# Moving VectorE work between units: one more added pair of q-k products, one more early set of down-weight sums, and a later deadline for V's sums

## The chip, the cores and the metric

The kernel runs on one NeuronCore of a Trainium2 chip. The metric is the device time of one execution in microseconds (us). Before the change the median of three runs is 715.35 us (715.16 to 716.04). A profile of one more execution comes with it; that execution took 715.07 us.

## The reference

Everything is bfloat16; x is 2048 rows of 1024 values. The output mixes an attention branch and a gated MLP branch row by row.

```python
g = _sigmoid((x * gate_w).sum(-1, keepdims=True))
# A: 32 heads of 32, each row looks at itself and 7 earlier rows, 2 apart
q, k, v = split(x @ wqkv)                       # wqkv 1024 x 3072
idx  = pos[:, None] - 2 * arange(8)[None, :]    # negative: masked with -1e9
logits = einsum("bhsd,bhswd->bhsw", q, k[idx]) * 32 ** -0.5
a = einsum("bhsw,bhswd->bhsd", softmax(logits), v[idx]) @ wo
# B: hidden width 3584
b = (gelu(x @ w_gate) * (x @ w_up)) @ w_down
return g * a + (1 - g) * b
```

## The kernel before

**Units.** The rows are handled as two halves `s` of 1024 rows. All projections of x are cut into 78 *units*. A unit makes two 128-column tiles of one projection for one half. It does so by a seven-product scheme (Strassen-Winograd): the 2 x 2 blocks of the weights and of x are combined by additions beforehand, and seven block products of four 128x512 matmuls each replace eight. So a unit is 28 matmuls, all issued by `Unit.mm` (L354). Units 2 to 9 make q and k of half 0, 10 to 17 q and k of half 1 (`t` counts eight tile pairs in each half, so unit 2 + 8s + t is the pair (s, t)), 18 to 25 make V, and 26 to 77 make gate and up. After unit 77 comes the down stage: two calls of `down`, in which TensorE works at L1074 and L1107.

**Order in a unit.** For unit b the main loop issues, to TensorE: product 1 of b, products 7 and 3 of unit b-1, product 5 of b, then a *slot* in which head sums may be made, products 2 and 6 of b, and last product 4 of unit b-1. VectorE adds product 5 to the banks that 7 and 3 left (L400, one instruction for each unit). Product 4 of the same unit accumulates into one of these banks, so TensorE can't start it before L400 is done.

**VectorE's background work.** Everything else on VectorE is handed out by a planner while the program is written (`bg`, `run_bg`, `due`). Each task is a generator that yields the cost in us of what it has just issued. In each unit the planner adds 4.7 (4.8 from unit 26 on) to a credit, plus 1.6 or 0.8 if the slot held reductions; what was left over carries on, at most 0.3 of it if positive, all of it if negative. It then steps the task with the lowest priority number whose time has come, as long as the credit is above 0.3. Tasks with the same number go in the order in which they were entered. `due(n, task)` and `at(n, fn)` run at the start of unit n, ahead of its L400, and charge nothing to the credit. So VectorE's order in unit b is: what is forced at its start, L400 of unit b-1, what `at_end` holds, and the planner's tasks.

**q-k products.** The task `qk_prods` (priority 2, from unit n+2 on, due at n+4 for a pair made in unit n) multiplies q by the eight shifted k for three blocks of 256 rows: two blocks in one instruction (L599, 4096 elements) if the credit is over 1.5, else one (L592, 2048 elements). When an odd t is done, the products of t-1 and t are summed over each head's 32 values on TensorE: `reduce_mm` (L604) issues four 128x512 matmuls with 32 columns of ones for each product, so 24 for a pair of tiles, in the slot of a later unit. For a pair in `ADDED` VectorE first adds the two tiles' products (L637: one instruction of 4096, one of 2048 elements), and 12 matmuls are enough; before, only the last pair, (1, 7), is there, as a task of priority 1.9. The products of the next pair start only when the reductions of the pair before are issued. `softmax` takes the head sums on VectorE in a front part (priority 1) and, after the exponential on ScalarE, `softmax_back` (priority 3: L726 sum, L728 reciprocal, L729, L731).

**Down-weight sums.** `t_forms` combines the down and output weights for the down stage in nine sets q of 2 k-tiles: one subtraction of 2048 elements (L892), two of 1024 (L895), and four stores of 256 KB through GpSimd's queue (L898). Set q is loaded by `tf_load` on the SP queue into `R_TF[q]`, an offset in KB in the one big SBUF tile `arena`. Sets 0 to 4 may be formed from units 2, 3, 6, 8 and 9 on, with priority 6; `tf_close` at the end of unit 13 forces what is left of them, sets the priority to 4.5 and issues `load_v`, V's weights, into 92 to 108 KB. Set 5 lies at 16 KB, is loaded at unit 19, may start at unit 20 and is forced by `tf_done` at unit 23; sets 6 to 8 come from unit 28 on. Other users of 16 to 24 KB are q's weights up to unit 17 and, from unit 24 on, `sums_pair` of the first gate and up weights (L314, priority 1, four instructions that each write 2 KB of it).

**V's sums.** `sums_v` (L540, priority 2, from unit 16) makes four weight sums of 2048 elements for V; it is due at unit 18.

Of the kernel before, what the change touches and what calls it, by code (L numbers as in the profile page):

```python
# [23 lines left out]
SJ = AC // NJ  # L24
# [10 lines left out]
R_Z = (194.5, 196.5)  # L35
R_ZH = 90
R_EX = (194.5, 81, 50, 81, 84)
R_ATTN = 73
R_E = 81
R_GW = 81  # L40
# [6 lines left out]
R_ST = 178  # L47
R_P5B = 198.5
R_RAW = (0, 8)
R_TF = (64, 92, 100, 108, 92, 16, 92, 100, 108)  # L50
R_S = (16, 24)
R_O = (36, 32)
R_VB = (40, 48.25)
# [9 lines left out]
def _win_ap(src: bass.AP, dims):  # L63
    return AP(src.tensor, src.offset, [list(src.ap[0])] + [list(d) for d in dims])
# [3 lines left out]
def kernel(  # L68
# [20 lines left out]
    NT = KT  # L89
# [12 lines left out]
    def reg(kb, n):  # L102
        o = int(kb * KB)
        return arena[:, o:o + n]

    def reg3(kb, a, b):
        return reg(kb, a * b).rearrange("p (a b) -> p a b", a=a)
# [4 lines left out]
    def regf(kb, n):  # L112
        return reg(kb, 2 * n).bitcast(F32)
# [23 lines left out]
    with tc.manual_schedule(engines={mybir.EngineType.PE, mybir.EngineType.DVE, mybir.EngineType.Activation,  # L137
# [63 lines left out]
        def flat(a):  # L201
            return a.rearrange("p a b -> p (a b)")
# [210 lines left out]
        now = [0]  # L413
# [17 lines left out]
        def bg(gen, prio, wake):  # L431
            t = Task(gen, prio, wake)
            tasks.append(t)
            tasks.sort(key=lambda t_: t_.prio)
            return t
# [41 lines left out]
        def at(n, fn):  # L477
            hooks.setdefault(n, []).append(fn)
# [7 lines left out]
        def due(n, t):  # L486
            at(n, t.finish)

        Q0 = 2
# [40 lines left out]
        def load_v():  # L530
            for k0 in (0, HK):
                nc.sync.dma_start(out=wv[:, k0:k0 + HK, :],
                                  in_=A_wqkv[k0 * P:(k0 + HK) * P, 2 * D:3 * D].rearrange("(k p) n -> p k n", p=P))

        def sums_v():
            L11, L12 = wv4[:, 0:HK, :, 0:4], wv4[:, HK:KT, :, 0:4]
            L21, L22 = wv4[:, 0:HK, :, 4:8], wv4[:, HK:KT, :, 4:8]
            for o_, a, b_, op in ((sv[0], L21, L22, ALU.add), (sv[1], sv[0], L11, ALU.subtract),
                                  (sv[2], L12, sv[1], ALU.subtract), (L21, L11, L21, ALU.subtract)):
                TT(out=o_, in0=a, in1=b_, op=op)  # L540
                yield 1.14

        def v_forms(t):
# [9 lines left out]
        NQKV = len(units)  # L553
# [18 lines left out]
        prod = [reg3(o, NWIN, AC) for o in pr_off]  # L572
        attn_all = reg3(R_ATTN, NBLK, SC)
        mask = reg3(R_MASK, NWIN, SJ)
# [11 lines left out]
        def prod_tile():  # L586
            k = pr_n[0] % 6
            pr_n[0] += 1
            return prod[k]

        def qk_mult(dst, q, k):
            TT(out=dst, in0=q.rearrange("p (o s) -> p o s", o=1).to_broadcast([P, NWIN, AC]),  # L592
               in1=_win_ap(k, [[-DIL, NWIN], [1, AC]]), op=ALU.mult)

        def pair_at(a, b):
            return _win_ap(reg(a, NWIN * AC), [[int((b - a) * KB), 2], [1, NWIN * AC]])

        def qk_mult2(dst, q, k, sq, sk):
            TT(out=dst, in0=_win_ap(q, [[sq, 2], [0, NWIN], [1, AC]]),  # L599
               in1=_win_ap(k, [[sk, 2], [-DIL, NWIN], [1, AC]]), op=ALU.mult)  # L600
# [4 lines left out]
                                 start=start, stop=stop)  # L605

        ND = BPS - 1
        ADDED = {(1, 7)}
        LGB = 5
        reduced, front, prods = [0], set(), {}  # L610

        def qk_prods(u, s, t):
            while reduced[0] < NT * s + t - t % 2:
                yield None
            assert ND == 3 and pr_n[0] % 3 == 0
            k = pr_n[0] % 6
            out_ = [prod_tile() for _ in range(ND)]
            a = 0
            while a < ND:
                if a == 0 and credit[0] > 1.5:  # L620
                    qk_mult2(pair_at(pr_off[k], pr_off[k + 1]), u.T[:, 0, 0:AC], u.T[:, 1, 0:AC], AC, AC)
                    a += 2
                    yield 2.21
                else:
                    qk_mult(out_[a], u.T[:, 0, a * AC:(a + 1) * AC], u.T[:, 1, a * AC:(a + 1) * AC])
                    a += 1
                    yield 1.14
            prods[t] = out_
            if (s, t) in ADDED:
                bg(qk_add(s, t), 1.9, now[0])  # L630
            elif t % 2:
                slotq.append((1.6, lambda: (qk_reduce(s, t - 1, prods[t - 1]), qk_reduce(s, t, out_))))

        def qk_add(s, t):
            for a, b in ((0, 3), (2, 5)):
                u, v = ((pair_at(pr_off[i], pr_off[i + 1]) if a == 0 else reg(pr_off[i], NWIN * AC)) for i in (a, b))
                TT(out=u, in0=u, in1=v, op=ALU.add)  # L637
                yield 2.21 if a == 0 else 1.14
            slotq.append((0.8, lambda: qk_reduce(s, t - 1, prods[t - 1], 2)))

        def qk_reduce(s, t, out_, m=1):
            assert s == 0 or t > 0 or front == {0, 2}
            for a, pr in enumerate(out_):
                reduce_mm(bank(LGB + a), pr, t == 0, t + m == NT)
            reduced[0] += m
            if t + m == NT:
                if s == 0:
                    bg(softmax(0, 2, LGB, 0), 1, now[0])
                    bg(softmax(2, 1, LGB + 2, 1), 1, now[0])
                else:  # L650
                    bg(softmax(BPS, 3, LGB, 2), 1, now[0])
# [42 lines left out]
        ready = set()  # L694
        md = consts.tile([P, 4, SJ], F32, name="md")

        def softmax(a, cnt, b0, e):
            ee = regf(R_EX[e], cnt * SC)
            e4 = ee.rearrange("p (a w s) -> p a w s", a=cnt, w=NWIN)
            sw = ee.rearrange("p (a w s) -> p a s w", a=cnt, w=NWIN)  # L700
            lg = banks[:, b0:b0 + cnt, :]
            src = lg.rearrange("p a (w s) -> p a w s", w=NWIN)
            bc = lambda t_: t_.rearrange("p a (o s) -> p a o s", o=1).to_broadcast([P, cnt, NWIN, SJ])
            if a == 0:
                TT(out=src[:, 0], in0=src[:, 0], in1=mask, op=ALU.add)
                yield 0.6
            m = md[:, (0, 2, 0, 3, 0)[e]:(0, 2, 0, 3, 0)[e] + cnt, :]
            assert e < 2 or ready >= {2: {0, 1, 2}, 3: {0, 1, 2}, 4: {4, 5, 6}}[e]
            V.tensor_reduce(out=m, in_=lg.rearrange("p a (w s) -> p a s w", w=NWIN), axis=AX.X, op=ALU.max)
            yield 0.55 * cnt + 0.05  # L710
            TT(out=e4, in0=src, in1=bc(m), op=ALU.subtract)
            yield 0.55 * cnt + 0.05
            front.add(a)
            actq.append(lambda: softmax_exp(a, cnt, ee, e4, sw, m, bc))
# [3 lines left out]
        def softmax_exp(a, cnt, ee, e4, sw, m, bc):  # L718
            nc.scalar.activation(out=ee, in_=ee, func=ACT.Exp, scale=scale)
            bg(softmax_back(a, cnt, ee, e4, sw, m, bc), 3, now[0] + 1)  # L720
# [91 lines left out]
        at_slot(Q0 + 8, lambda: (gate_chunk(3, bank(1)), bg(gate_task(1), 0, Q0 + 8)))  # L812
        due(Q0 + NT + 1, bg(late_form3(), 1, Q0 + 8))
        TFE = Q0 + 12
        due(Q0 + 2 * NT, bg(sums_v(), 2, TFE + 2))
        for s in range(2):
            for t in range(NT):
                n_ = Q0 + NT * s + t
# [44 lines left out]

        NP = 2
        NQ = NK // NP
        N1, N2 = 5, 6
        TB = Q0 + 2 * NT + 1
        TC = NQKV + 1

        def tf_set(q):  # L870
            return [reg3(R_TF[q] + NP * k, NP, SC) for k in range(4)]

# [8 lines left out]
        def t_forms():  # L881
            for q in range(NQ):
                tf_q[0] = q
                if q in (N1, N2):
                    tft.prio = 3.9 if q == N1 else 4.5
                    tasks.sort(key=lambda t_: t_.prio)
                while now[0] < (Q0 + (0, 1, 4, 6, 7)[q] if q < N1 else 1 + (TB if q < N2 else TC)):
                    yield None
                r11, r12, r21, r22 = tf_set(q)
                n_ = NP * SC  # L890
                both = _win_ap(flat(r11), [[n_, 2], [1, n_]])
                TT(out=both, in0=_win_ap(flat(r12), [[2 * n_, 2], [1, n_]]), in1=both, op=ALU.subtract)  # L892
                yield 1.14
                for o_, a, b_ in ((r22, r22, r11), (r21, r21, r22)):
                    TT(out=flat(o_), in0=flat(a), in1=flat(b_), op=ALU.subtract)  # L895
                    if o_ is r21:
                        for k, t in enumerate((r11, r22, r12, r21)):
                            nc.gpsimd.dma_start(out=t_d[k][:, NP * q:NP * q + NP, :], in_=t)  # L898
                    yield 0.61

        for q, b in ((2, 2), (3, 4), (4, 5)):
            at(Q0 + b, lambda q=q: tf_load(q))
        at(TB, lambda: ([tf_load(q) for q in range(N1, N2)], spill_load(1)))
        at(TC, lambda: [tf_load(q) for q in range(N2, NQ)])
# [3 lines left out]
            while tf_q[0] < N2:  # L908
                tft.step()

        at(NQKV - 3, tf_done)

        def tf_close():
            while tf_q[0] < N1:
# [362 lines left out]
        def head():  # L1277
            xs, f = xf[0], []
            for i, o in enumerate((R_ATTN, R_PROD)):
                for m in range(2):  # L1280
# [122 lines left out]
```

## Time and profile before

| | |
|---|---|
| median of 3 runs | 715.35 us |
| the profiled execution, its time | 715.07 us |
| its span in the profile | 713.3 us |
| TensorE (PE) busy | 704.4 us, 99% of the span |
| VectorE (DVE) busy | 671.6 us, 94% |
| ScalarE (ACT) busy | 329.9 us, 46% |
| GpSimd (POOL) busy | 143.5 us, 20% |
| granted TensorE clock | 1.0 |

The span is the time from the first to the last instruction of the program; 1.8 us of the execution lie around it. In the profile, a line number such as L400 is the line of the kernel that issued the instruction; a count x12 says how many instructions were merged; what stands after `idle before` or `<-` is what ended a wait. Start times are from the start of the span. TensorE's matmuls overlap, so their mean duration (379 ns) is longer than the distance from one to the next; the distances are taken from the start times of the weight loads (PEld), of which each matmul has one.

### The profile page before, as it was taken

Reading aid. Unit: us, or ns where it says so; the run is one execution under the profiler, and the core shown is the slowest. Engines: PE = TensorE matmul, PEld = TensorE weight load, DVE = VectorE, ACT = ScalarE, POOL = GpSimd, SP = SyncE. Lnnn points to the kernel's source line nnn. Section 1 sums busy time; section 2 is a strip of 40 time slices with the busy share of each in tenths; the row PEclk is TensorE's granted clock in tenths of the full one; section 3 lists DMA queues with packets and bytes.
Section 4 is the critical chain, followed back from the end, with each engine's and each line's share of the span. In section 5 each row is a group of like instructions: output and inputs, shape, how many; then the busy total and the mean of one; then the engine's idle time right before and its main releaser. Section 6 shows DMA issues by size and latency. Waiting matters only on the chain.

```text
span 713.3 us, 10651 instructions
## 1 busy us (share of the span) xinstructions
PE 704.4 (99%) x4033; PEld 406.9 (57%) x4089; DVE 671.6 (94%) x631; ACT 329.9 (46%) x602; POOL 143.5 (20%) x248
## 2 busy tenths in 40 slices
PE   8999999999999999999999999999999999999998
PEld 4466666655544444444444444444447886758887
DVE  3989989989999999999999999999699999799997
ACT  5554445445466665555555555555322321132431
POOL 1243445222502442222210110101110002100011
PEclk9999999999999999999999999999999999999999
DMA  9989351394475758665753764464951899995951
GB/s 299 324 217 284 134 201 42 99 259 142 150 250 166 257 180 270 201 218 165 236 179 118 252 210 142 146 259 148 428 228 40 307 402 393 420 428 223 400 214 60
DMA packets 94755, 162.03 MB, mean 227 GB/s; under 512 B 23680, under 2 KB 71200, under 8 KB 90352
## 3 DMA queue, kind: packets, MB, share of 16 engines
q1 hardware_dynamic: 77632, 105.46, 43.0%
q0 software_dynamic: 16352, 48.29, 19.7%
q10 hardware_dynamic: 720, 7.60, 2.8%
q8 instruction: 32, 0.52, 0.3%
q14 instruction: 19, 0.16, 0.1%
HBM read 112.17 MB, written 54.14 MB: 233 GB/s over the span
## 4 chain that ended last, share of the span: by engine, by line
PE 95%; DVE 3%; issue 1%; DMA 1%; SPq 0%; DVEq 0%
PE banks L354 65%; PE banks L1074 19%; PE banks L1107 9%; PE banks L604 2%; DVE arena L400 1%; DMA arena<-in_A_x_dram 1%; DVE arena L314 0%; DVE arena L774 0%; DVE arena L222 0%; DVE arena L768 0%; PE banks L273 0%; DVE arena L1288 0%; DVE arena L248 0%; DVE arena L892 0%; DVE arena L245 0%
## 5 line engine op out<-in xcount | busy, mean ns | idle before, releaser
L354 PE MATMUL banks<-arena 128*128 128x512 bf16 x2191 | 484.6, 379 | 3.8 <-DVE ones_r L261 0.4
L354 PEld LDWEIGHTS <-arena 128*128 128x128 bf16 x2240 | 245.7, 110 | 240.7 <-issue 6.4
L1074 PE MATMUL banks<-arena 128*128 128x256 bf16 x1260 | 138.3, 273 | 0.0
L1074 PEld LDWEIGHTS <-arena 128*128 128x128 bf16 x1260 | 123.3, 98 | 15.2 <-issue 0.3
L381 ACT COPY arena<-banks 128x512 f32<-128x512 f32 x80 | 46.9, 587 | 129.8 <-PE banks L354 129.8
L400 DVE TENSOR_TENSOR arena<-banks,arena 128x1024 bf16<-128x1024 f32 x80 | 97.5, 1219 | 7.9 <-ACT arena L408 3.6
L362 ACT CAST arena<-banks 128x512 bf16<-128x512 f32 x104 | 60.9, 585 | 43.0 <-PE banks L354 42.7
L768 DVE TENSOR_TENSOR arena<-arena 128x4096 bf16<-128x4096 bf16 (+1 forms) x40 | 73.6, 1860 | 0.3
L774 DVE TENSOR_TENSOR arena<-arena 128x2048 bf16<-128x2048 bf16 (+2 forms) x53 | 68.0, 1283 | 1.0
L251 POOL DMA_DIRECT2D h_d<-arena x28 | 20.3, 729 | 216.4 <-DVE arena L245 142.6
L1107 PE MATMUL banks<-arena 128*128 128x512 bf16 x281 | 62.4, 379 | 0.4
L389 ACT COPY banks<-banks 128x512 f32<-128x512 f32 x80 | 45.6, 570 | 22.0 <-PE banks L354 20.4
L1032 DVE TENSOR_TENSOR arena<-arena 128x2304 bf16<-128x2304 bf16 x40 | 53.3, 1354 | 0.5
L376 ACT COPY banks<-banks 128x512 f32<-128x512 f32 x80 | 46.1, 576 | 14.4 <-PE banks L354 13.2
L599 DVE TENSOR_TENSOR arena<-arena 128x4096 bf16<-128x4096 bf16 x22 | 50.1, 2284 | 0.1
L1079 ACT COPY banks<-banks 128x256 f32<-128x256 f32 x60 | 21.4, 356 | 61.8 <-PE banks L1074 61.6
L1107 PEld LDWEIGHTS <-arena 128*128 128x128 bf16 x288 | 28.1, 98 | 33.6 <-DMA arena<-h_d 0.3
L360 ACT ACTIVATE arena<-banks 128x512 bf16<-128x512 f32 x56 | 33.4, 597 | 20.1 <-PE banks L354 20.1
L955 DVE TENSOR_TENSOR arena<-arena 128x2048 bf16<-128x2048 bf16 (+1 forms) x40 | 41.8, 1116 | 0.4 <-DMA arena<-h_d 0.4
L1040 DVE TENSOR_TENSOR arena<-arena 128x2304 bf16<-128x2304 bf16 x28 | 37.8, 1355 | 0.2
L245 DVE TENSOR_TENSOR arena<-arena 128x2048 bf16<-128x2048 bf16 x28 | 34.0, 1217 | 2.8 <-ACT arena L362 2.8
L314 DVE TENSOR_TENSOR arena<-arena 128x1024 bf16<-128x1024 bf16 x56 | 36.1, 686 | 0.5
(92 smaller groups left out, 453.6 us busy)
## 6 DMA issues: line engine op xcount, KB each, us to landing
arena<-t_d SPq DMA_DIRECT2D x8, 2304.0 KB, 10.2
h_d<-arena POOLq DMA_DIRECT2D x28, 512.0 KB, 4.9
arena<-w_c SPq DMA_DIRECT2D x12, 1152.0 KB, 13.4
t_d<-arena POOLq DMA_DIRECT2D x36, 256.0 KB, 4.9
arena<-h_d SPq DMA_DIRECT2D x6, 1536.0 KB, 13.0
arena<-in_B_w_down_dram SPq DMA_DIRECT2D x28, 256.0 KB, 7.0
r_d<-arena ACTq DMA_DIRECT2D x3, 2304.0 KB, 8.7
arena<-r_d SPq DMA_DIRECT2D x3, 2304.0 KB, 14.2
```

What stands on the lines that cost most here:

```text
L354: self.pe = nc.tensor.matmul(ps, lhsT=self.L[form](kt), rhs=rhs[:, kt, :], start=(start and kt == 0), stop=(kt == HK - 1), skip_group_chec ...
L362: nc.scalar.copy(out=o_, in_=i_)
L376: nc.scalar.copy(out=self.Y, in_=self.X)
L381: nc.scalar.copy(out=self.p5s, in_=self.V)
L389: nc.scalar.copy(out=self.Z, in_=self.Y)
L400: TT(out=self.T[:, :, c2s], in0=pair, in1=self.p5s.rearrange("p (o n) -> p o n", o=1).to_broadcast([P, 2, SC]), op=ALU.add)
L599: TT(out=dst, in0=_win_ap(q, [[sq, 2], [0, NWIN], [1, AC]]), in1=_win_ap(k, [[sk, 2], [-DIL, NWIN], [1, AC]]), op=ALU.mult)
L768: TT(out=prod2[:, t % 4:t % 4 + m, :], in0=flat(ab).rearrange("p (o n) -> p o n", o=1).to_broadcast([P, m, NWIN * AC]), in1=_win_ap(v[:, t ...
L774: TT(out=h(0) if w > 1 else o_[:, t:t + m, :], in0=h(0), in1=h(1), op=ALU.add)
L1032: TT(out=o_, in0=a, in1=b_, op=op)
L1074: nc.tensor.matmul(c(i, h, j), lhsT=l[:, kt, j * P:(j + 1) * P], rhs=r[:, kt, :], start=False, stop=(kt == KH - 1), skip_group_check=True)
L1107: nc.tensor.matmul(ps, lhsT=L[:, i, j * P:(j + 1) * P], rhs=R[:, i, :], start=(start and q == 0), stop=(q == NK - 1), skip_group_check=not ...
```

## The change

Four things, and what has to move for them:

- `ADDED` gets a second pair, (1, 1): the products of units 10 and 11. The add now runs inside the `qk_prods` task, for (1, 7) too (priority 2 in place of 1.9).
- Set 5 of the down-weight sums joins the early sets (`N1` 5 to 6, `N2` 6 to 7): loaded at unit 9 into 100 KB, where set 2 was, allowed from unit 11 on, and so inside what `tf_close` forces at the end of unit 13, ahead of `load_v`. Set 6 takes over the place at 16 KB, the load at unit 19 and the start at unit 20; `tf_done` forces it at unit 24 in place of 23. Sets 7 and 8 remain for unit 28 and later. The line that sets the priority now stands behind the wait.
- At unit 18 only the first two of V's four sums are forced; the rest at unit 19.
- The softmax of the last three-block group (`e == 2`) keeps its maxima at 72 KB of `arena` and no longer needs the earlier softmax parts to be finished.

```diff
+R_MD = 72
-R_TF = (64, 92, 100, 108, 92, 16, 92, 100, 108)
+R_TF = (64, 92, 100, 108, 92, 100, 16, 92, 100)
...
+        sv_n = [0]
+
         def sums_v():
...
                 TT(out=o_, in0=a, in1=b_, op=op)
+                sv_n[0] += 1
                 yield 1.14
...
-        ADDED = {(1, 7)}
+        ADDED = {(1, 1), (1, 7)}
...
             if (s, t) in ADDED:
-                bg(qk_add(s, t), 1.9, now[0])
+                yield from qk_add(s, t)
...
-            m = md[:, (0, 2, 0, 3, 0)[e]:(0, 2, 0, 3, 0)[e] + cnt, :]
-            assert e < 2 or ready >= {2: {0, 1, 2}, 3: {0, 1, 2}, 4: {4, 5, 6}}[e]
+            m = regf(R_MD, 3 * SJ).rearrange("p (a s) -> p a s", a=3) if e == 2 else md[:, (0, 2, 0, 3, 0)[e]:(0, 2, 0, 3, 0)[e] + cnt, :]
+            assert e < 3 or (2, 0)[e - 3] in ready
...
-        due(Q0 + 2 * NT, bg(sums_v(), 2, TFE + 2))
+        sv_task = bg(sums_v(), 2, TFE + 2)
+        at(Q0 + 2 * NT, lambda: [sv_task.step() for _ in range(2 - sv_n[0])])
+        due(Q0 + 2 * NT + 1, sv_task)
...
-        N1, N2 = 5, 6
+        N1, N2 = 6, 7
...
                 tf_q[0] = q
+                while now[0] < (Q0 + (0, 1, 4, 6, 7, 9)[q] if q < N1 else 1 + (TB if q < N2 else TC)):
+                    yield None
                 if q in (N1, N2):
                     tft.prio = 3.9 if q == N1 else 4.5
                     tasks.sort(key=lambda t_: t_.prio)
-                while now[0] < (Q0 + (0, 1, 4, 6, 7)[q] if q < N1 else 1 + (TB if q < N2 else TC)):
-                    yield None
...
-        for q, b in ((2, 2), (3, 4), (4, 5)):
+        for q, b in ((2, 2), (3, 4), (4, 5), (5, 7)):
             at(Q0 + b, lambda q=q: tf_load(q))
...
-        at(NQKV - 3, tf_done)
+        at(NQKV - 2, tf_done)
```

Here Q0 is 2, NT 8, NQKV 26, TB 19, TC 27 and TFE 14.

## The prediction

> **What bounds the kernel now.** I read the page's busy times first, then the groups by shape for prices, then the chain and the two engines' timelines between 90 and 260 us, where the edits lie.
>
> ```profile
> PE 704.4 (99%) x4033; PEld 406.9 (57%) x4089; DVE 671.6 (94%) x631; ACT 329.9 (46%) x602; POOL 143.5 (20%) x248
> ```
>
> TensorE leaves 8.9 us of the span. A gain is matmuls taken away or one of its few pauses; a loss is a new pause. Prices:
>
> ```profile
> L592 DVE TENSOR_TENSOR arena<-arena 128x2048 bf16<-128x2048 bf16 x20 | 24.3, 1220 | 1.8 <-DMA h_d<-arena 1.8
> L895 DVE TENSOR_TENSOR arena<-arena 128x1024 bf16<-128x1024 bf16 x18 | 12.4, 690 | 0.4
> L604 PE MATMUL banks<-arena,ones_r 128*32 128x512 bf16 x196 | 12.4, 381 | 0.0
> L892 DVE TENSOR_TENSOR arena<-arena 128x2048 bf16<-128x2048 bf16 x9 | 11.0, 1220 | 0.0
> L540 DVE TENSOR_TENSOR arena<-arena 128x2048 bf16<-128x2048 bf16 x4 | 4.8, 1223 | 0.1
> ```
>
> The second line of prices is distances in the VectorE timeline: independent instructions follow each other every 1.14 us (2048 elements), 2.20 (4096) and 0.61 (1024). The chain shows how VectorE delays TensorE: a down-weight sum stands ahead of the add L400, and matmuls resume only behind that.
>
> ```profile
> 237.97 5.30 PE banks L354 x24
> ...
> 243.67 1.22 DVE arena L892
> 244.88 1.15 DVE arena L400
> ...
> 246.07 9.87 PE banks L354 x45
> ```
>
> From the trace's single weight loads I took each unit's start and its *lag*: the start of L400 minus the start of product 5. A unit without a slot lasts 6.04 us, product 5 starts 2.59 after the unit and product 4 another 2.59 later. The lag is 0.47 where VectorE waits for the matmuls. Units with lags 1.53, 1.65, 1.71, 1.76 and 1.93 (68, 59, 23, 74, 34) lost 0, 0.12, 0.18, 0.23 and 0.39 us: loss = lag - 1.53, and a slot adds its own length to that tolerance. Next the VectorE timeline:
>
> ```profile
> 79.06 1.22 DVE L892 TENSOR_TENSOR arena<-arena 128x2048 bf16<-128x2048 bf16 x1
> 80.31 1.42 DVE L895 TENSOR_TENSOR arena<-arena 128x1024 bf16<-128x1024 bf16 x2
> 81.65 1.22 DVE L400 TENSOR_TENSOR arena<-banks,arena 128x1024 bf16<-128x1024 f32 x1
> ...
> 176.38 1.22 DVE L400 TENSOR_TENSOR arena<-banks,arena 128x1024 bf16<-128x1024 f32 x1
> 177.52 2.84 DVE L726 TENSOR_REDUCE md<-arena 128x192 f32<-128x1536 f32 x1
> 180.39 1.35 DVE L728 RECIPROCAL md<-md 128x192 f32<-128x192 f32 x1
> 181.78 0.36 DVE L729 TENSOR_TENSOR md<-md,gblk 128x192 f32<-128x192 f32 x1
> 182.06 1.22 DVE L400 TENSOR_TENSOR arena<-banks,arena 128x1024 bf16<-128x1024 f32 x1
> 183.19 2.61 DVE L314 TENSOR_TENSOR arena<-arena 128x1024 bf16<-128x1024 bf16 x4
> ```
>
> The reader should see that a whole set of down-weight sums takes 2.59 us (79.06 to 81.65), and that in unit 23 VectorE is full from one L400 to the next. Last, TensorE's timeline: a pair's reductions, and an added pair's.
>
> ```profile
> 121.90 1.48 PE L604 MATMUL banks<-arena,ones_r 128*32 128x512 bf16 x24
> ...
> 162.84 0.83 PE L604 MATMUL banks<-arena,ones_r 128*32 128x512 bf16 x12
> ```
>
> **The change, part by part.** I wrote the planner's credit down unit by unit; for the kernel before it gives the order that the timeline has in every unit that I compared. End credits are in brackets.
>
> *Twelve matmuls fewer.* Unit 15, with the 24 of pair (1, 1), lasted 7.61 us; unit 21, with 12, 6.96. Gain 0.65.
>
> *Set 5 early.* Unit 11 has 5.00 of credit and 3.35 of work, and VectorE then idles 1.48 us. L892 and the first L895 go there [-0.10]; L400 of unit 12 moves from 101.50 to 101.9, and behind it VectorE waits for reductions at 103.30 as before: nothing lost. Cover gone, 1.9 us. The second L895 is forced in unit 13, not charged, and moves L400 of unit 14 from a lag of 1.09 to 1.70: loss 0.17. The four loads wait on SP for set 2's stores (last landed 84.8) and are needed at 99.9. The four stores go onto GpSimd's queue at 112.6 to 114.2 and put off the gate's small stores by 2.1 us; their reader comes at 181.78. V's second load, issued at 99.50 and landed 8.6 us later before, waits for these stores until 117, lands by 126 and is needed at 129.6: hidden, with 4 us of cover.
>
> *The add of (1, 1).* 3.34 us in unit 14, in front of softmax's L726 [-0.75]; L400 of unit 15 falls to 122.9, a lag of 2.0, which its slot covers. Unit 15 has only 0.8 for its slot: products of (1, 2) leave 1.40, under the 1.5 for a double, so (1, 3) starts with a single one [0.26]. In unit 16 V's four sums come first, being entered earlier with the same priority, then one more product [-0.74]. The third is forced at the start of unit 17. On VectorE: L400 at 128.5, sums to 134.4, products to 135.55 and 136.8. Unit 17's slot begins at 134.8; its first 20 reductions take 1.2, and the last four wait until 136.8. Loss 0.8. No run shows this wait; if the product is in time it is 0, and with queue latency 1.0. I take 0.8, the distance of the rows.
>
> *V's sums.* By the ledger all four are issued in unit 16, as before: the later deadline does nothing. *Maxima at 72 KB:* same instruction, nothing.
>
> *Set 6.* Before, set 5's L892 found credit in unit 20. Now unit 20 holds the add (3.35) and softmax parts pushed out of 14 and 18 (1.25) [-0.14]; unit 21 the softmax front and a product [-0.25]; 22 two doubles [0.03]; 23 softmax's 4.70 [0.03]. So set 6 is forced whole at unit 24. VectorE catches up by unit 23 (lag 0.47); L400 to L400 there is 5.68 (176.38 to 182.06), plus 2.59, minus 6.04: lag 2.70, loss 1.17.
>
> *Its place.* Right behind that L400 come the four L314, which write 16 to 24 KB, where set 6 is being stored. Before, set 5's stores landed at 179.98 and L314 began at 183.19. Now the stores are issued at 182.4 to 184.2, and set 5's needed 2.5 to 2.9 us: the four parts come free from 185.0 to 187.1, while L314 would run from 184.9 to 187.4. About 1.1 us more. Between 0 (each part just in time) and 2.2 (all wait for the last). That VectorE waits for a store is seen in the row of L592 above. Then unit 25: 2.70 + 6.46 (L400 to L400 before) + 1.1 - 6.04 - 1.17 = lag 3.05, loss 1.52, where 0.06 was lost.
>
> *What goes away.* The two L895 forced at unit 23 (0.18), set 6's work in units 32 and 33 (0.39 at unit 34), 0.05 at unit 31. Afterwards VectorE is some 2 us ahead. The two later pauses (0.12 at 59, 0.23 at 74) depend on how instructions fall into units; I keep their sum, between -0.35 and +0.4. SP's loads at unit 27 are eight in place of twelve, hidden.
>
> **Sum.** -0.65 + 0.17 + 0.8 + 1.17 + 1.46 - 0.18 - 0.39 - 0.05 = +2.3 us. The profiled execution becomes 717.4. It stood 0.28 below the median, so the median becomes 717.7, 0.33% above. About 0.2% (1.43 us) is what a measurement of this kernel can tell from no change.
>
> **Rivals.**
> - *Set 6 is formed out of the budget by unit 22* (this ends on the other side: not slower). It decides at unit 20: 0.45 more credit, or the softmax part done a unit earlier, and L892 goes there as it did at 161.01. Against it: the ledger. Then units 24 and 25 lose nothing: 717.7 - 2.6 = 715.1. Chance 0.18. With both other pauses, too, absent it is 714.1; the pauses before and the slot hold only 1.85 us in all, so over 0.2% faster gets 0.04.
> - *Half of the pauses are smaller*: product (1, 3) in time, L314 not held: 717.7 - 0.8 - 1.1 = 715.8. Chance 0.09.
> - *V's weights come late*: if the stores and the load take over 4 us longer than before, L540 holds L400, the products and unit 17's slot. DMA has room there (7 to 9% busy from 106 to 118 us). 2 us beyond that point: 719.7. Chance 0.05.
> - *TensorE's clock falls after the pauses.* The granted clock is 1.00 in every stretch from 92 to 253 us, with the 0.61 us gap at 246 in it. At the start eight matmuls took 3.53 us in place of 1.75, so 1.8 for each of three pauses: 723. Chance 0.02. The Trainium skill, "TensorE: Matmul & The Clock Gate", Part 1, lets the clock halve after an idle window of about 3.4 us, and its section on psum-queue depth-cycling warns that frequent micro-idles do it as well. By the first the pauses here are too short and the sum stays; by the second it would be this rival; the trace's many small pauses at 1.00 speak for the first.
>
> **Numbers.** The forecast has 0.62, with its own range 716.6 to 718.8 from 0 to 2.2 at L314; unit 17 (0 to 1.0) and the later pauses lie in the whole range. Slower: 0.60 of it, V's weights, the clock, and a little of the smaller pauses: 0.69. No change: 0.27. Faster: 0.04. The range 715.1 to 718.9 leaves out the clock, late weights and the faster tail.
>
> **What would show it.** Right: L604 x12 near 122 us; three gaps of TensorE near 136, 184 and 190 us; L892 with two L895 directly ahead of an L400 near 181 us; L314 idle before it with a DMA to t_d as its end; L540 still one run of four. Wrong: L892 of set 6 near 161 to 175 us, no idle time at L314, or the reductions in unit 17 running through. The forecast fails if the credit ledger is off by half a microsecond at unit 20.

## The result and the profile after

The changed kernel takes 717.37 us (median of 22 runs, 716.91 to 722.68) against 715.35 us for the kernel before in 22 runs beside it. The ratio is 1.0032, with a 95% interval of 1.0022 to 1.0042: slower by about 2 us. The profiled execution took 717.09 us, with a span of 715.3 us.

In the changed kernel the line numbers move by a few: the matmuls of a unit are L355 (L354 before), the add of product 5 is L401 (L400), the head reductions L608 (L604), products of 2048 elements L596 (L592), V's sums L543 (L540), the down-weight sums L898 and L901 (L892, L895), and the first gate sums L315 (L314).

From the page, the busy times, and of the groups the one that holds the units' matmuls (its last number is the idle time of TensorE just before them):

```profile
PE 707.6 (99%) x4077; PEld 407.2 (57%) x4077; DVE 674.8 (94%) x633; ACT 330.0 (46%) x602; POOL 143.5 (20%) x248
```

```profile
L355 PE MATMUL banks<-arena 128*128 128x512 bf16 x2240 | 487.6, 379 | 3.2 <-DVE arena L401 2.7
```

VectorE has 3.2 us more to do, the added pair's L641. TensorE waits for the add L401 before its matmuls. The waits of TensorE and then those of VectorE (who waited <- for whom: us in all, times, longest) name three places:

```profile
PE banks L355 <- DVE arena L401: 2.7, 2, 1.7
PE banks L608 <- DVE arena L596: 0.3, 1, 0.3
```

```profile
DVE arena L315 <- DMA t_d<-arena: 1.2, 1, 1.2
```

TensorE's timeline shows when (start, us, what, and in brackets the idle time before it):

```profile
121.86 0.83 PE L608 MATMUL banks<-arena,ones_r 128*32 128x512 bf16 x12
...
134.86 1.26 PE L608 MATMUL banks<-arena,ones_r 128*32 128x512 bf16 x20
136.46 0.40 PE L608 MATMUL banks<-arena,ones_r 128*32 128x512 bf16 x4 [0.33 <-DVE arena L596]
...
184.54 6.20 PE L355 MATMUL banks<-arena 128*128 128x512 bf16 x28 [1.02 <-DVE arena L401]
192.41 10.67 PE L355 MATMUL banks<-arena 128*128 128x512 bf16 x48 [1.67 <-DVE arena L401]
```

The gain is in the first line: 12 reductions at 121.86 where 24 stood. The loss is in the other rows: a wait inside the reductions of unit 17, and one pause each for units 24 and 25. VectorE's timeline around them:

```profile
129.26 4.88 DVE L543 TENSOR_TENSOR arena<-arena 128x2048 bf16<-128x2048 bf16 x4
134.05 2.35 DVE L596 TENSOR_TENSOR arena<-arena 128x2048 bf16<-128x2048 bf16 x2
...
180.68 1.22 DVE L898 TENSOR_TENSOR arena<-arena 128x2048 bf16<-128x2048 bf16 x1
181.93 1.42 DVE L901 TENSOR_TENSOR arena<-arena 128x1024 bf16<-128x1024 bf16 x2
183.27 1.22 DVE L401 TENSOR_TENSOR arena<-banks,arena 128x1024 bf16<-128x1024 f32 x1
184.53 0.69 DVE L315 TENSOR_TENSOR arena<-arena 128x1024 bf16<-128x1024 bf16 x1
186.41 2.00 DVE L315 TENSOR_TENSOR arena<-arena 128x1024 bf16<-128x1024 bf16 x3 [1.19 <-DMA t_d<-arena]
...
191.14 1.22 DVE L401 TENSOR_TENSOR arena<-banks,arena 128x1024 bf16<-128x1024 f32 x1
```

Set 6 of the down-weight sums stands whole and directly ahead of an L401 (180.68 to 183.27). Behind it L315 waits 1.19 us for set 6's stores, because it writes where they still read. And V's four sums are still one run of four, ahead of the two products that unit 17's reductions need.

Taken unit by unit from the weight loads, the 76 units from unit 2 to unit 77 take 476.70 us in place of 474.46: +2.24. The down stage is unchanged (206.37 and 206.38), and the stretch before unit 2 is 0.20 shorter.

### The profile page after: what moved, and what is told of

The parts are those of the page before. It is cut to its first block, busy times and chain, and to the rows that moved or that the text cites. A ratio compares the mean times of both kernels' runs of the same rounds, so it can differ in the third digit from the quotient of the medians.

```text
span 715.3 us, 10694 instructions
## 1 busy us (share of the span) xinstructions
PE 707.6 (99%) x4077; PEld 407.2 (57%) x4077; DVE 674.8 (94%) x633; ACT 330.0 (46%) x602; POOL 143.5 (20%) x248
## 4 chain that ended last, share of the span: by engine, by line
PE 73%; DVE 0%; issue 0%
PE banks L355 45%; PE banks L1080 19%; PE banks L1113 9%; DVE arena L401 0%; PE banks L608 0%; DVE arena L1237 0%
## 5 line engine op out<-in xcount | busy, mean ns | idle before, releaser
L355 PE MATMUL banks<-arena 128*128 128x512 bf16 x2240 | 487.6, 379 | 3.2 <-DVE arena L401 2.7
L355 PEld LDWEIGHTS <-arena 128*128 128x128 bf16 x2240 | 245.8, 110 | 242.4 <-issue 8.7
L401 DVE TENSOR_TENSOR arena<-banks,arena 128x1024 bf16<-128x1024 f32 x80 | 97.5, 1220 | 7.3 <-PE banks L355 6.5
L778 DVE TENSOR_TENSOR arena<-arena 128x2048 bf16<-128x2048 bf16 (+2 forms) x52 | 67.8, 1304 | 0.9
L1038 DVE TENSOR_TENSOR arena<-arena 128x2304 bf16<-128x2304 bf16 x40 | 53.3, 1354 | 0.5
L603 DVE TENSOR_TENSOR arena<-arena 128x4096 bf16<-128x4096 bf16 x21 | 47.9, 2285 | 0.2 <-ACT arena L382 0.2
L961 DVE TENSOR_TENSOR arena<-arena 128x2048 bf16<-128x2048 bf16 (+1 forms) x40 | 41.7, 1114 | 0.0
L1046 DVE TENSOR_TENSOR arena<-arena 128x2304 bf16<-128x2304 bf16 x28 | 37.8, 1355 | 0.3
L315 DVE TENSOR_TENSOR arena<-arena 128x1024 bf16<-128x1024 bf16 x56 | 36.2, 686 | 1.7 <-DMA t_d<-arena 1.2
L246 DVE TENSOR_TENSOR arena<-arena 128x2048 bf16<-128x2048 bf16 x28 | 34.0, 1217 | 2.8 <-ACT arena L363 2.8
```

Of the source, the lines that this page charges most:

```text
L355: self.pe = nc.tensor.matmul(ps, lhsT=self.L[form](kt), rhs=rhs[:, kt, :], start=(start and kt == 0), stop=(kt == HK - 1), skip_group_chec ...
L401: TT(out=self.T[:, :, c2s], in0=pair, in1=self.p5s.rearrange("p (o n) -> p o n", o=1).to_broadcast([P, 2, SC]), op=ALU.add)
L603: TT(out=dst, in0=_win_ap(q, [[sq, 2], [0, NWIN], [1, AC]]), in1=_win_ap(k, [[sk, 2], [-DIL, NWIN], [1, AC]]), op=ALU.mult)
L778: TT(out=h(0) if w > 1 else o_[:, t:t + m, :], in0=h(0), in1=h(1), op=ALU.add)
```

## The experiments

The theory under test: set 6 is forced because the budget of VectorE is used up by the add of (1, 1), and every pause is an instruction that stands ahead of an L401 or a reduction. Two rivals. *More work*: VectorE simply has 3.3 us too much before unit 25, in whatever order. *Collision*: the place at 16 KB, shared with L315, makes both late pauses. All runs are compared with the kernel before on the same chip; its medians there were 715.2 to 715.6. The sum over the units is of the profiled execution. The line numbers are those of the changed kernel.

### Another place for set 6

```diff
-R_TF = (64, 92, 100, 108, 92, 100, 16, 92, 100)
+R_TF = (64, 92, 100, 108, 92, 100, 24, 92, 100)
```

> The changed kernel with set 6 of the down-weight sums at 24 KB in place of 16 KB, so that the first gate and up sums (four instructions in unit 24) no longer write where set 6 is still being stored; nothing else moves. Theory of forced work (VectorE's add comes late where work is forced ahead of it, and the loss is the lag less 1.53 us): the 1.19 us wait for the store goes, unit 24 still loses 1.2, unit 25 loses about 0.4 in place of 1.83; span 1.4 us shorter than the changed kernel's 715.3, median about 716.0, ratio to before 1.001. Rival 'collision' (the shared place is the whole loss at units 24 and 25): both pauses go, 714.4. Rival 'more work' (VectorE simply has 3.3 us more to do): as the changed kernel, ratio 1.003.

Measured: 716.03 us, ratio 1.0000 (0.9991 to 1.0009); the units take 475.26. VectorE's timeline, and then TensorE's:

```profile
183.60 1.22 DVE L401 TENSOR_TENSOR arena<-banks,arena 128x1024 bf16<-128x1024 f32 x1
184.74 2.61 DVE L315 TENSOR_TENSOR arena<-arena 128x1024 bf16<-128x1024 bf16 x4
...
190.07 1.21 DVE L401 TENSOR_TENSOR arena<-banks,arena 128x1024 bf16<-128x1024 f32 x1
```

```profile
184.87 6.20 PE L355 MATMUL banks<-arena 128*128 128x512 bf16 x28 [1.02 <-DVE arena L401]
191.34 10.67 PE L355 MATMUL banks<-arena 128*128 128x512 bf16 x47 [0.26 <-DVE arena L401]
```

L315 runs through, and L401 follows L401 after 6.47 us in place of 7.87. The second pause falls from 1.67 to 0.26; the first stays at 1.02. So the collision costs 1.40 us and is only the second pause. The first is the forced set.

### Set 6 allowed earlier, and V's sums behind the products

Three runs. In the changed kernel the down-weight sums wait for unit 20 at priority 4.5 and get 3.9 only once they have been reached, so `spill` (4) and `pv_all` (4.2) go first. In the first run `tf_close` gives them 3.9 at once; in the second, V's sums get priority 2.1, behind the products; the third has both.

```diff
-            tft.prio = 4.5
+            tft.prio = 3.9
             tasks.sort(key=lambda t_: t_.prio)
             load_v()
```

```diff
-        sv_task = bg(sums_v(), 2, TFE + 2)
+        sv_task = bg(sums_v(), 2.1, TFE + 2)
```

> The changed kernel with the priority 3.9 given to the down-weight sums already at the end of unit 13, so that set 6 is formed out of the credit in units 21 and 22, ahead of the spill products, and nothing of it is forced at unit 24. The same VectorE work in all. Theory of forced work: no pause at units 24 and 25 (1.18 and 1.83 us gone), the pauses at 14 (0.17) and 17 (0.51) stay; span about 712.5, median 714.5, ratio 0.999. Rival 'more work': ratio stays at 1.003. Rival 'collision': the pauses go too, so this run does not part it from the theory; e1_place does.

> The changed kernel with V's four sums at priority 2.1 in place of 2, so that the products of pair (1, 3) go ahead of them in unit 16 and none is forced at unit 17. Theory of forced work: unit 17 loses nothing in place of 0.51 us, V's fourth sum moves to unit 18 and nothing waits for it, the pauses at 24 and 25 stay; span about 714.8, median 716.9, ratio 1.0025. Rival 'more work': as the changed kernel, 1.003.

> The edits of e2_prio and e3_vsums together: same work, nothing of set 6 forced at unit 24, no product forced at unit 17. Theory of forced work: only the pause of 0.17 us at unit 14 is left of the new ones and the slot's 0.65 us are a net gain; span about 712.0, median about 714.1, ratio 0.998, faster than both kernels. Rival 'more work': 1.003.

Measured: set 6 earlier 715.83, ratio 0.9998 (0.9988 to 1.0008). V's sums later 718.5, ratio 1.0033 (1.0021 to 1.0044). Both 715.19, ratio 0.9985 (0.9975 to 0.9996). Each edit removed the pause that it was aimed at. With the first, units 24 and 25 lose nothing. With the second, unit 17 loses 0 in place of 0.52 (and unit 24 1.51 in place of 1.18), since its products now stand ahead of V's sums; VectorE's timeline of that run:

```profile
129.40 2.34 DVE L596 TENSOR_TENSOR arena<-arena 128x2048 bf16<-128x2048 bf16 x2
131.66 3.73 DVE L543 TENSOR_TENSOR arena<-arena 128x2048 bf16<-128x2048 bf16 x3
```

In the run with set 6 earlier, VectorE's timeline has set 6 in unit 21, out of the budget:

```profile
167.47 1.22 DVE L898 TENSOR_TENSOR arena<-arena 128x2048 bf16<-128x2048 bf16 x1
168.72 0.69 DVE L901 TENSOR_TENSOR arena<-arena 128x1024 bf16<-128x1024 bf16 x1
169.38 1.22 DVE L401 TENSOR_TENSOR arena<-banks,arena 128x1024 bf16<-128x1024 f32 x1
```

But all three missed the expected time by 1.1 to 1.6 us, and in the main for one reason (the second run also for the 0.33 more at unit 24, where the lag was 3.04 in place of 2.71): units 76 and 77, which lose nothing before or after the change, now lose about 0.31 and 1.04. VectorE's timeline of the run with both:

```profile
500.76 1.22 DVE L246 TENSOR_TENSOR arena<-arena 128x2048 bf16<-128x2048 bf16 x1 [1.73 <-ACT arena L363]
502.01 1.22 DVE L249 TENSOR_TENSOR arena<-arena,omgrep 128x2048 bf16<-128x2048 bf16 x1
503.16 1.82 DVE L952 TENSOR_TENSOR arena<-arena,omgrep 128x2048 bf16<-128x2048 bf16 x2
504.90 1.22 DVE L401 TENSOR_TENSOR arena<-banks,arena 128x1024 bf16<-128x1024 f32 x1
```

L952 scales a block of h for the down stage (A21, priority 6, allowed five units before the end). Two of its instructions have come to stand behind L246, which multiplies gate and up and waits there for ScalarE, and ahead of an L401. The budget knows no waiting: it counted both as fitting. I had not put this into the expectations; moving work at unit 20 changes what is left over 50 units later.

### The scale of A21 after the last unit

The kernel with both priorities, and the changed kernel, each with the scale allowed only from unit 78 on:

```diff
-            bg(scale_task(Bs(s)["A21"], s, 1, 0, KX), 6, n - 5)
+            bg(scale_task(Bs(s)["A21"], s, 1, 0, KX), 6, n)
```

> The kernel with both priorities changed (set 6 ahead, V's sums behind the products), and the scale of block A21, which the down stage needs, is allowed only after unit 77 in place of five units earlier. Its three instructions then stand behind the last L401, where VectorE otherwise waits 3.17 us for the last load of h. Theory that the two scale instructions in unit 77 make the pauses at 76 and 77: both go, 1.36 us, the span becomes 711.9 and the median 713.8, ratio 0.9965 to 0.997 against the kernel before. Rival, the pauses come from ScalarE's late output (the 1.73 us wait of VectorE in unit 77): they stay at least by 0.7, 714.5 to 715.2, ratio 0.9985. Third: the scale is now late for the down stage, which begins up to 2 us later, and the gain is given back: 715 to 716.

> The changed kernel with the late scale of A21 alone. There units 76 and 77 have no pause, so nothing is to be gained: 717.2 to 717.5, ratio 1.003, by either theory of the pauses at 24 and 25. It shows whether the late scale itself costs the down stage something: 0 if the three instructions fit into VectorE's 3.17 us of idle time there, up to 2 us more (719.4) if not.

Measured: with both priorities 714.25, ratio 0.9991 (0.9982 to 0.9999); units 472.97. The pauses at 76 and 77 are gone, 1.37 us as the theory had it, but the down stage takes 206.87 in place of 206.44. The changed kernel with this edit alone is unmoved: 717.19, ratio 1.0026 (1.0015 to 1.0037), units 476.63, with the same pauses at 17, 24 and 25; its down stage stays at 206.37, so there the late scale costs nothing.

### One part of the change at a time

First, without the second added pair; second, with that pair alone, the sets of down-weight sums as before.

```diff
-        ADDED = {(1, 1), (1, 7)}
+        ADDED = {(1, 7)}
```

```diff
-R_TF = (64, 92, 100, 108, 92, 100, 16, 92, 100)
+R_TF = (64, 92, 100, 108, 92, 16, 92, 100, 108)
...
-        N1, N2 = 6, 7
+        N1, N2 = 5, 6
...
-        for q, b in ((2, 2), (3, 4), (4, 5), (5, 7)):
+        for q, b in ((2, 2), (3, 4), (4, 5)):
...
-        at(NQKV - 2, tf_done)
+        at(NQKV - 3, tf_done)
```

> The changed kernel without the second added pair: pair (1, 1) is reduced with 24 matmuls again; the early set 5 and everything else of the change stay. Forced work: with the 3.34 us of the add out of unit 14, the parts of softmax are no longer pushed into unit 20, so set 6's large instruction finds credit there and its two small ones in unit 21; nothing is forced at unit 24. Units 24 and 25 go back to the kernel before (1.18 and 1.77 us against the changed kernel), unit 17 too (0.52), unit 15 loses its 0.65; what stays is +0.17 at unit 14 and -0.17 at 23, -0.05 at 31, -0.39 at 34, about -0.5 against the kernel before: 714.9 to 715.1, ratio 0.999. If two scale instructions of the down stage fall into unit 77 as in the runs with another priority, 1.36 more. Rival, set 6's place at 16 KB alone is the cause: the pauses at 24 and 25 stay, 717.5 to 718, ratio 1.003.

> The kernel before with the add of pair (1, 1) alone (and the maxima at 72 KB): the sets of down-weight sums are loaded, placed and forced as before. Forced work: unit 15 keeps its gain of 0.65, unit 17 loses 0 to 0.5 (the third product of (1, 3) is still forced there), set 5 is late by one unit in units 20 and 21 but is not forced, so no pause at 24 and 25 and none of 0.18 at 23: -0.3 to -0.8 against the kernel before, 714.6 to 715.3, ratio 0.999; 1.36 more if the scale instructions of the down stage are moved into unit 77. Rival, the add is the cause by itself (3.3 us more of VectorE work before V): pauses of about 1.2 and 1.8 at units 24 and 25, as in the changed kernel, 717.4, ratio 1.003.

Measured: without the add 715.81, ratio 1.0005 (0.9997 to 1.0014); the add alone 716.33, ratio 1.0011 (0.9997 to 1.0025). Neither has a pause at unit 24 or 25. Without the add, set 6 does find credit in unit 20, where parts of softmax (L732 to L735) stand in the changed kernel. VectorE's timeline of the changed kernel first, then without the add:

```profile
157.59 3.42 DVE L641 TENSOR_TENSOR arena<-arena 128x4096 bf16<-128x4096 bf16 x2
160.93 0.55 DVE L732 RECIPROCAL md<-md 128x64 f32<-128x64 f32 x1
161.51 0.23 DVE L733 TENSOR_TENSOR md<-md,gblk 128x64 f32<-128x64 f32 x1
161.77 0.69 DVE L735 TENSOR_TENSOR arena<-arena,md 128x512 bf16<-128x512 f32 x1
162.38 1.22 DVE L401 TENSOR_TENSOR arena<-banks,arena 128x1024 bf16<-128x1024 f32 x1
```

```profile
158.50 3.42 DVE L641 TENSOR_TENSOR arena<-arena 128x4096 bf16<-128x4096 bf16 x2
161.84 1.22 DVE L898 TENSOR_TENSOR arena<-arena 128x2048 bf16<-128x2048 bf16 x1
162.97 1.22 DVE L401 TENSOR_TENSOR arena<-banks,arena 128x1024 bf16<-128x1024 f32 x1
```

With the add alone, unit 17's third product is in time, but one more product (L596, at 142.11) then stands ahead of the next L401, and unit 18 loses 0.75, which I had placed in unit 17. TensorE's timeline of that run:

```profile
134.53 1.48 PE L608 MATMUL banks<-arena,ones_r 128*32 128x512 bf16 x24
135.94 7.99 PE L355 MATMUL banks<-arena 128*128 128x512 bf16 x36
144.51 4.48 PE L355 MATMUL banks<-arena 128*128 128x512 bf16 x20 [0.59 <-DVE arena L401]
```

Both runs carry the pause at 76 and 77 (1.34 and 1.35), which hides what the parts are worth. So I ran both, and the kernel before, with the late scale of A21.

> The kernel before with the late scale of A21 alone. It has no pause at units 76 and 77 to win back, so it shows what the late scale costs by itself: three VectorE instructions, 2.9 us, move behind the last L400. In the combined kernel the down stage then grew by 0.5 us. Theory that this growth comes from VectorE's instructions: 0 to +0.5 us, 715.4 to 715.9, ratio 1.000 to 1.0007. Rival, the late scale is itself a gain in any kernel: 714.2, ratio 0.998.

> The changed kernel without the second added pair, with the late scale of A21: the same kernel as the run without the add, but without the 1.34 us at units 76 and 77. Theory that these two instructions made that pause: units come out 0.5 below the kernel before (unit 5 apart, which waits for a transfer that differs from one execution to the next), the down stage 0 to 0.5 above: 714.6 to 715.2, ratio 0.9985 to 0.9995. Rival, the pause has another cause: 715.8, ratio 1.0005.

> The kernel before with the add of pair (1, 1) alone and the late scale of A21. Without the 1.35 us at units 76 and 77 there remain -0.65 at unit 15, +0.75 at unit 18, -0.17 at 23, -0.4 at 33 and 34, -0.3 at 59 and 74: units about 0.7 below the kernel before, the down stage 0 to 0.5 above: 714.7 to 715.3, ratio 0.9985 to 0.9995. Rival, the add costs the kernel time in whatever company: 716.3, ratio 1.001.

Measured: the kernel before with the late scale 715.69, ratio 0.9998 (0.9987 to 1.0010), units 474.43; without the add 715.12, ratio 0.9993 (0.9981 to 1.0005), units 473.66; the add alone 715.02, ratio 0.9989 (0.9976 to 1.0002), units 473.76. Against the 474.43 the parts gain 0.77 and 0.67 in the units; the two together with both priorities gain 1.46 (472.97). The same two as the change orders them lose 2.20 (476.63). So the rival "more work" falls: the same work on VectorE, in another order, costs nothing. That 1.46 is close to the sum of the parts is chance. Both parts win the same 0.9 us, at units 23, 34, 59 and 74, which the two together win only once; and the add alone loses 0.76 at unit 18, which the two together don't lose. The medians alone can't tell either part from no change, since both intervals hold 1; what the parts are worth rests on the sums over the units, which repeat: the same pause came out within 0.03 us in every profile that has it, but for what unit 5 waits (last section).

The down stage took 207.3 to 207.5 us in these three kernels in place of 206.4. That I expected as 0 to 0.5 from VectorE's own instructions; it was up to 1.1. TensorE's timeline without the add shows a wait of the down stage itself:

```profile
539.60 35.69 PE L1080 MATMUL banks<-arena 128*128 128x256 bf16 x324
576.16 19.82 PE L1080 MATMUL banks<-arena 128*128 128x256 bf16 x180 [0.88 <-DVE arena L1046]
```

### The scale of A21 ahead of the wait

Last, the kernel with both priorities, with the scale in front of L246 rather than after the last unit:

```diff
-            bg(scale_task(Bs(s)["A21"], s, 1, 0, KX), 6, n - 5)
+            bg(scale_task(Bs(s)["A21"], s, 1, 0, KX), -1, n - 2)
```

> The kernel with both priorities changed, and the scale of A21 put at the front of VectorE's work from unit 76 on: its three instructions stand in one run ahead of the instruction L246 that waits there for ScalarE, in place of one in unit 75 and two behind that wait. By the distances of the rows they take 2.9 us at most in a gap of 2.9 (1.14 of the instruction that leaves unit 75, and the wait of 1.73). Theory that these instructions make the pauses at 76 and 77 only because they stand behind the wait: both pauses go, 1.36 us, as with the late scale, and nothing is pushed into the down stage, which stays at 206.4: span 711.8 to 712.0, median 713.6 to 713.9, ratio 0.9965 to 0.998. Rival, VectorE is too full there in any order: the pauses stay in part, 714.5 to 715.2, ratio 0.9985.

Measured: 715.08, ratio 0.9984 (0.9965 to 1.0003); units 473.00, so both pauses go again. Three instructions fit into the time in which VectorE waited for ScalarE. But the span missed by 1.6 us: the stretch ahead of unit 2 was 0.7 longer in this execution (33.12), and the down stage took 207.44. VectorE's timeline names what it waits for; below it the same places in the kernel before, where L774 and L955 are L778 and L961:

```profile
495.48 1.94 DVE L778 TENSOR_TENSOR arena<-arena 128x2048 bf16<-128x2048 bf16 x2
...
498.48 2.95 DVE L952 TENSOR_TENSOR arena<-arena,omgrep 128x2048 bf16<-128x2048 bf16 x3
501.35 1.22 DVE L246 TENSOR_TENSOR arena<-arena 128x2048 bf16<-128x2048 bf16 x1
...
531.68 1.29 DVE L961 TENSOR_TENSOR arena<-arena 128x1024 bf16<-128x1024 bf16 x2 [4.91 <-DMA arena<-h_d]
```

```profile
490.88 0.68 DVE L774 TENSOR_TENSOR arena<-arena 128x1024 bf16<-128x1024 bf16 x1
...
527.94 1.29 DVE L955 TENSOR_TENSOR arena<-arena 128x1024 bf16<-128x1024 bf16 x2 [0.38 <-DMA arena<-h_d]
```

The load of h from memory lets L961 go at 531.68; it was 527.94 in the kernel before, 530.69 with both priorities alone, and 530.28, 531.26 and 531.41 in the three changed kernels with the late scale whose down stage grew. What VectorE combines from it (L1038, L1046) is later, and TensorE waits 0.9 us for L1046 near 576 us. Here the scale does not stand behind the last unit, so the down stage need not have the late scale to become longer. Of the 1.46 us that the units gain, a third (the late scale: 0.49) to three quarters (here: 1.06) is given back in the down stage.

Shorter units are not what makes the load late. VectorE waits 1.5 to 4.9 us for it in nine of the fourteen profiles, among them the first run without the add, whose units are longer than before (475.83): 4.2 us. What the nine have in common is where attention ends on VectorE: its last addition (L778) is done at 496.6 to 500.0 us, against 491.56 in the kernel before and 487.70 in the changed kernel. In all fourteen, SP issues its next loads of h 0.02 to 0.04 us behind that addition. In the run above the DMA engines move nothing from 487 to 497 us, where their busy share was 0.45 in the kernel before, and are still busy from 527 to 531 us (0.95 in place of 0.05); GpSimd's four loads of h, issued behind them, take up to 16.8 us in place of 11.2. So the edits have moved attention's end too, and with it the start of these loads. This is read from the traces; no run moved attention's end alone.

How much of it TensorE feels depends on when the units end. Counted from the end of unit 77, L961 goes after at most 24.3 us in the runs with a late load whose down stage grows by under 0.1, after 24.8 and 25.0 where it grows by 0.32 and 0.49, and after 25.4 to 25.6 where it grows by 0.94 to 1.10. This suggests that in the run with both priorities alone the pauses at 76 and 77 hid the late load.

The three kernels with both priorities have ratios of 0.9985, 0.9991 and 0.9984, all against 1.0032 for the change as it is. Two of their intervals lie below 1; the runs can't rank the three.

## Why the prediction was right

It said 717.7 us and slower; measured 717.37.

- *Twelve matmuls fewer, -0.65.* Unit 15 went from 7.61 to 6.96 us. Right.
- *Set 5 early, +0.17 at unit 14, the loads, the stores and V's load hidden.* Unit 14 lost 0.17 with the lag of 1.70 that was forecast, and V's sums show no wait. Right.
- *The rule loss = lag - 1.53.* In the fourteen profiles VectorE's add makes 59 losses of 0.02 us or more in units without a slot, up to a lag of 3.37, and the rule gives each within 0.01 us. Right, and most terms below rest on it.
- *Unit 17, 0.8.* The mechanism was right, the size was not: the last four reductions waited 0.33 us, and the unit grew by 0.52 (splitting the 24 cost the other 0.19). The mis-sized term is the time of the products. I had them end at 136.8, from an L400 at 128.5; the L401 there started at 128.12, and they ended at 136.40 (134.05 + 2.35). With V's sums behind them the loss is 0, as the second priority run showed.
- *V's sums do nothing.* One run of four in unit 16, as the ledger had it. Right for the deadline; the priority, not the deadline, decides where they stand.
- *Set 6 forced at unit 24, 1.17.* Measured 1.18, lag 2.71 against 2.70. The run with another place kept this loss, and those where set 6 found credit earlier did not have it. Right.
- *Its place, 1.1 us of waiting, 1.52 lost in unit 25.* L315 waited 1.19 us in the timeline, but the cost of the place is 1.40 (7.87 against 6.47 between the two L401), and unit 25 lost 1.83. The mis-sized term is the wait for the stores: I let the first part come free just in time (at 185.0, for an L315 at 184.9), and the trace shows a first L315 that starts 1.26 us behind its L401 in place of 1.14, so it waited too.
- *What goes away, -0.18, -0.39 and -0.05.* Measured -0.17, -0.39, -0.05. Right.
- *Later pauses kept.* Those at 59 and 74 were gone (-0.12, -0.22), three small ones of 0.19 in all came at 44, 53 and 55: -0.15, inside the range given. That these are a matter of how work falls into units was right, and larger than I took it for: up to 1.36 in the experiments.

Unit 17 was 0.28 too high and unit 25 0.31 too low, so that the close sum is partly luck. None of the rivals came about. The clock stayed up: the windows of the trace (us, then busy time and instructions of PE, PEld, DVE, ACT and POOL, the granted clock, DMA share, GB/s) give 1.00 over the stretch that holds both pauses.

```profile
182.00:200.00 18.00, 15.31 (x71) 8.38 (x69) 16.71 (x14) 8.69 (x15) 11.75 (x21) 1.00 0.52 169
```

The Trainium skill, "TensorE: Matmul & The Clock Gate", Part 1, puts the idle window after which the clock falls at about 3.4 us; pauses of 1.02 and 1.67 us with the clock at 1.00 agree with it.

## What to carry to other kernels

Forced work costs what it puts ahead of the instruction that another engine waits for: take the lag at that place, subtract the tolerance, and follow it to the next unit. A planner that counts costs but not waits can be pushed into a pause far from the edit, so test an edit's parts under the same order of the later work before calling a part dear. And before a buffer's place is moved, look at who writes there next and how long the stores before it need.

## What was not expected of the hardware

The load of h at the start of the down stage is the next limit. In the kernel before it is hidden (VectorE waits 0.38 us for it); in the nine kernels whose attention ends later VectorE waits up to 4.91 us, and TensorE up to 0.9 where the units are short as well. In the kernel before with the late scale alone VectorE doesn't wait for it, but TensorE itself waited 0.86 us for a part of h, near 524 us, and the down stage took 207.41. Why that part was late stays open.

The same code waits differently for a transfer from one execution to the next: unit 5, untouched in every kernel, was delayed by 0.86 us in the profiled execution without the add and by 0.17 in the one with set 6 earlier, and by 0 in the others. In the first VectorE waited 2.31 us for a DMA there, in the kernel before 1.75.
